# A filter transposed by DMAs out of DRAM and laid out through a DRAM scratch, in place of TensorE and SBUF transposes; first units in narrower column pieces; a new order

## The chip, the cores and the metric

The kernel runs on one core of one Trainium2 chip. The metric is the device time of one execution in microseconds (us), as the median of several runs. Times on the profiled execution are counted from the start of its span. PE is TensorE, DVE is VectorE, ACT is ScalarE, POOL is GpSimd, and SP is the engine that issues most of the DMAs. SP, like every engine, works through its own instructions in order: an instruction that waits holds up all that stand behind it on that engine.

## What is computed

All tensors are bf16. `S` is 2048 time steps and `D` is 512 channels; the hidden width of the gated block is 1792.

```python
xn = layernorm(A_q)                                   # over D
k_shift[s] = sum over j<4 of A_k[s-j] * A_shift_k[:, j]
kv = k_shift * A_v
y  = causal convolution over time of kv with A_ssm_k  # by FFT of length 2S, each channel its own filter
y  = y + kv * A_ssm_D
g  = silu( (gelu(xn @ w_gate) * (xn @ w_up)) @ w_down )
out = A_q + (xn * y) * g
```

`A_ssm_k` is the filter: 512 channels by 2048 time steps in DRAM, a row per channel. All other long inputs have a row per time step.

## The kernel before, in words

**The convolution.** Time step s is split as 16 p + t: p is the partition (128 of them), t one of 16 slots. A first stage (`stage1_h`, `stage1_k`; the matmuls with F1 at L618) transforms over the partitions for each t: two 128x128 weights per slot of 512 channels. Its result is written to a DRAM scratch, ZH for the filter and ZK for kv, and read back regrouped (BH, BK). A second stage (`h_stage2`, `spectrum`, 32x32 tiles at L1028) completes the transform, multiplies the two spectra on DVE (L1091; HS and HW are the filter's spectrum and its swapped copy), transforms back and writes ZI. The last stage reads ZI as BI and multiplies with G1.

**The filter's way into the first stage.** The first stage needs the filter with a row per time step. `load_h` loads the filter as it lies in DRAM, four DMAs of 512 KB into Hn, one for each 128 channels. Two of the four are turned by PE: `h_transpose` (L878) transposes 32-bit pairs of elements against the identity ident32, and ACT or DVE copies the result from PSUM to HTr (L609, L612). The other two are permuted by ACT into HP (L609, four instructions) and then turned by two DMA transposes from SBUF to SBUF, HTD<-HP at L899, issued by SP. So the filter has two halves from here on, "H" and "J", with 16 stores of 256 KB to ZH: those of H are issued by ACT, those of J by SP. `half1` (eight pieces of 256 columns) serves the upper slots of the H half. The staging tiles of these stores lie in X and G.

**The gated block.** The time steps are done in four quarters q of 512 rows (slots 4q to 4q+3). `ln` does the statistics on DVE (L821, L822), the root on POOL (L831, L832) and the normalised rows XN on DVE (L835). `xn_transpose` turns them to xnT: for q 0 and 1 by PE (L854) with a copy by ACT, for q 2 and 3 by DMA (L846). `unit(q, m)` does hidden block m of 128: four matmuls with Wg and four with Wu over 512 columns, a gelu on ACT (L1137) and a product on DVE (L1140) to HT. For q = 0 and m below N_HALF = 2 the unit is done in two pieces of 256 columns (L1128, L1130). `down(q)` multiplies HT with Wd.

**What sets the order.** Each step is a task, added by `S.add` (or `op`), and numbered in the order in which the code adds it. The string SEQ is the order in which the tasks are emitted, written as these numbers; a "b" chooses the second engine of a task that has a choice. Each engine so gets its instructions in the order of SEQ, and PE and SP wait where their data is not there yet. ORDER only sets in what sequence the load tasks are numbered. Waits follow from overlapping reads and writes of the same memory (`Trk`); `after=` adds to them in the plan. The constants in `Sched` and LOAD_NS belong to the plan alone.

The weights Wg and Wu come in four pieces (units 0 and 1, 2 to 5, 6 to 9, 10 to 13). x01 and x11 are the loads of slots 0 and 1 of A_q, x22 that of slots 2 and 3, x1 to x3 those of the later quarters. PE begins with 11 matmuls on zeros (`warm_up`), before the first data lands.

Of the kernel before, what the change touches and what calls it, by code (L numbers as in the profile page):

```python
# [6 lines left out]
BF16 = mybir.dt.bfloat16  # L7
# [6 lines left out]
S_LEN = 2048  # L14
# [11 lines left out]
ORDER = "x01 h0 x11 h1 x22 w0 w1 h2 h3 D0 w2 s0 k0 v0 x1 w3 k1 v1 d0 d1 k2 v2 k3 v3 x2 x3"  # L26
SEQ = (
# [25 lines left out]
LOAD_NS = {("x0_", 262144): 1400.0, ("x0_", 131072): 450.0, 262144: 900.0, 524288: 1350.0, ("x", 524288): 2100.0, ("h", 524288): 1300.0, ("wg", 524288): 1550.0, ("wu", 524288): 1450.0, 917504: 2620.0, ("sk", 524288): 1500.0, 344064: 1250.0, 46080: 350.0, 3072: 100.0, 1024: 200.0}  # L53
W_XT, W_SW, W_BK, W_BH, W_ZI, W_BI, W_ZK, W_MI, W_G1 = 1665000, 600000, 555000, 703000, 333000, 640000, 490000, 740000, 222000
NC_PAIRS = 4
SMALL = 1.15 * 262144
T_FWD = 219.0
T_INV = 438.0
N_HALF = 2
# [232 lines left out]
class Sched:  # L292
# [10 lines left out]
    EARLY, TAKEN, SHARED, WAIT = (0.0, 1.0), 1400.0, 46000.0, 3300.0  # L303
    LANDS = (3150.0, 3490.0, 5770.0)
# [40 lines left out]
    def run(self):  # L345
# [5 lines left out]
        for name in SEQ.split():  # L351
# [13 lines left out]
            if eng == "loads":  # L365
                free[eng] = t.start + dur * (self.EARLY[1] if t.start < self.EARLY[0] else 1.0)
                if n_loads < len(self.LANDS):
                    free[eng] = self.LANDS[n_loads] - self.LOAD_LAT
                n_loads += 1
                t.end = free[eng] + self.LOAD_LAT  # L370
            elif t.nbytes:
                en = t.end
                if en < self.SHARED:
                    free["loads"] += self.TAKEN
                pipe = max(pipe, en + self.DMA_LAT / 2) + t.nbytes / (self.SHARE_BW if en < self.SHARED else self.DMA_BW)
                t.end = pipe + self.DMA_LAT / 2 + (self.WAIT if en < self.SHARED else 0.0)
# [22 lines left out]
def build_kernel(nc, A_q, A_k, A_v, A_shift_k, A_ssm_k, A_ssm_D, B_w_gate, B_w_up, B_w_down, out):  # L399
    with ExitStack() as es0:  # L400
# [31 lines left out]
        ident32 = new("ident32", [128, 128], FP32)  # L432
# [49 lines left out]
        def quarter(T, j):  # L482
            return T[:, j:j + 2, :].rearrange("p x (y d) -> p (x y) d", d=256).rearrange("p (r c) d -> p r c d", c=2)
# [42 lines left out]
        R_id, R_id32 = res("ident", ident[:]), res("ident32", ident32[:])  # L526
# [8 lines left out]
        R_AST = {x: [res(f"AST{x}{j}", a) for j, a in enumerate(ast[x])] for x in "HJK"}  # L535
# [8 lines left out]
        R_Hn = [res(f"Hn{k}", Hn[:, k, :]) for k in range(KD)]  # L544
        R_HTr = [[res(f"HTr{t}_{k}", HTr[:, t, 256 * k:256 * (k + 1)]) for k in range(2)] for t in range(NT // 2)]
        R_HP = [res(f"HP{h}", HP[:, 8 * h:8 * h + 8, :, :]) for h in range(2)]
# [740 lines left out]
```

## Time and profile before

| | us |
|---|---|
| median of 3 runs (lowest, highest) | 196.97 (196.69, 197.29) |
| the profiled execution's own time | 195.77 |
| its span | 194.0 |
| PE busy in the span | 187.5 |
| DVE, ACT, POOL busy | 159.8, 125.5, 14.0 |
| end of PE's warm-up on zeros | 5.84 |
| end of PE's last matmul | 190.25 |

"Busy" is the time in which an engine had at least one instruction under way. The span leaves out 1.77 us of the execution's own time, ahead of its first and behind its last instruction. In rows by line, the last columns are the busy time, the mean ns of one instruction and the idle time of its engine just before them. In rows of the timeline, the first two columns are the start and the length of a run of like instructions, and "x8" is how many. In rows of the windows, each engine has its busy time and its count; the last three columns are the granted clock, the mean busy share of the 16 DMA engines (over 1 where transfers overlap) and the GB/s that they moved. The granted clock is 1.00 in every window of this execution.

### The profile page before, as it was taken

What the parts mean: (1) busy time and instruction counts of PE and PEld (TensorE: products, weight loads), DVE (VectorE), ACT (ScalarE), POOL (GpSimd) and SP (SyncE); (2) the same over time, 40 slices, a digit from 0 to 9 for tenths busy, and PEclk for the clock granted to TensorE, in tenths of its full rate; (3) what the DMA queues carried; (4) which work ended last, traced back from release to release, by engine and by line L of the source; (5) the groups of instructions that cost most, each with busy time, mean ns of one, the idle gap of its engine ahead of it and who ended that gap; (6) DMA issues with size and microseconds to landing.
All of it is one profiled execution on the core that took longest, in us unless ns stands there. A gap on an engine that the chain in (4) does not pass through costs nothing.

```text
span 194.0 us, 3492 instructions
## 1 busy us (share of the span) xinstructions
PE 187.5 (97%) x1364; PEld 85.0 (44%) x1377; DVE 159.8 (82%) x245; ACT 125.5 (65%) x170; POOL 14.0 (7%) x32
## 2 busy tenths in 40 slices
PE   7799999999998999999999999999999999999993
PEld 2594544444443444443434433433444434444442
DVE  7599699998999993977788789878897963588993
ACT  6787999979876978868648767756577531222121
POOL 6412420000000000020300000000000000000000
PEclk9999999999999999999999999999999999999999
DMA  5999999999999859999999991893714344939333
GB/s 165 327 322 349 377 403 315 188 217 375 368 363 355 242 210 231 384 345 283 277 306 221 318 312 41 291 332 106 237 37 184 105 150 135 402 109 363 126 139 135
DMA packets 46102, 49.19 MB, mean 254 GB/s; under 512 B 12803, under 2 KB 39943, under 8 KB 46086
## 3 DMA queue, kind: packets, MB, share of 16 engines
q1 hardware_dynamic: 37510, 42.67, 69.8%
q10 hardware_dynamic: 8576, 6.29, 10.1%
q8 instruction: 11, 0.18, 0.4%
q14 instruction: 5, 0.04, 0.1%
HBM read 27.39 MB, written 14.68 MB: 217 GB/s over the span
## 4 chain that ended last, share of the span: by engine, by line
PE 87%; DMA 7%; ACT 2%; issue 1%; SPq 1%; DVE 1%
PE psall L618 80%; PE psall L1028 5%; DMA Hn<-in_A_ssm_k_dram 3%; DMA ZH<-X 3%; SPq L590 1%; PE psall L854 1%; ACT G L609 1%; PE psall L878 1%; ACT X L609 1%; ACT ASX L609 0%; ACT GE L1137 0%; DVE G L1175 0%; DVE G L1174 0%; ACT G L1172 0%
## 5 line engine op out<-in xcount | busy, mean ns | idle before, releaser
L618 PE MATMUL psall<-xnT,Wu 128*128 128x512 bf16 (+1 forms) x232 | 55.8, 372 | 0.0
L618 PE MATMUL psall<-xnT,Wg 128*128 128x512 bf16 (+1 forms) x232 | 55.3, 372 | 0.0
L618 PE MATMUL psall<-Wd,HT 128*128 128x512 bf16 (+2 forms) x231 | 50.8, 366 | 0.7 <-issue 0.5
L1140 DVE TENSOR_TENSOR HT<-psall,GE 128x512 bf16<-128x512 f32 x54 | 36.7, 685 | 15.2 <-PE psall L618 13.6
L1137 ACT ACTIVATE GE<-psall 128x512 bf16<-128x512 f32 x54 | 31.7, 601 | 12.6 <-PE psall L618 12.2
L618 PEld LDWEIGHTS psall<-Wd,HT 128*128 128x128 bf16 x238 | 22.4, 98 | 25.9 <-issue 1.1
L618 PEld LDWEIGHTS psall<-xnT,Wu 128*128 128x128 bf16 x232 | 21.6, 98 | 25.9 <-issue 3.8
L618 PEld LDWEIGHTS psall<-xnT,Wg 128*128 128x128 bf16 x232 | 21.9, 98 | 25.3 <-issue 1.3
L609 ACT ACTIVATE X<-psall 128x1024 bf16<-128x1024 f32 (+1 forms) x18 | 15.1, 846 | 3.8 <-DMA ZH<-X 3.3
L609 ACT ACTIVATE HS<-psall 128x1024 bf16<-128x1024 f32 x14 | 13.7, 1022 | 4.2 <-PE psall L1028 4.2
L1164 ACT ACTIVATE G<-psall 128x512 bf16<-128x512 f32 x12 | 7.0, 597 | 12.8 <-PE psall L618 12.4
L1011 DVE TENSOR_TENSOR KAC<-KAC,KTM 128x2048 bf16<-128x2048 bf16 x12 | 14.6, 1218 | 0.1
L1009 DVE TENSOR_TENSOR KTM<-KK,SKB 128x2048 bf16<-128x2048 bf16 x12 | 14.6, 1217 | 0.0
L609 ACT ACTIVATE BO<-psall 128x1024 bf16<-128x1024 f32 x9 | 9.1, 1023 | 8.2 <-PE psall L1028 7.7
L821 DVE BATCH_NORM_STATS2 stats<-X 128x6 f32<-128x512 bf16 x16 | 10.3, 677 | 3.9 <-DMA X<-in_A_q_dram 3.9
L609 ACT ACTIVATE KB<-psall 128x1024 bf16<-128x1024 f32 x11 | 11.0, 1021 | 3.6 <-PE psall L1028 3.6
L609 ACT ACTIVATE AST<-psall 128x1024 bf16<-128x1024 f32 x12 | 12.3, 1031 | 1.2 <-PE psall L618 1.0
L612 DVE CAST BO<-psall 128x1024 bf16<-128x1024 f32 x7 | 8.5, 1223 | 3.7 <-PE psall L1028 3.7
L1172 ACT ACTIVATE G<-psall 128x512 bf16<-128x512 f32 (+2 forms) x5 | 2.6, 512 | 13.1 <-PE psall L618 13.1
L1091 DVE TENSOR_TENSOR HW<-KB,HW 128x1024 bf16<-128x1024 bf16 x16 | 10.9, 682 | 0.0
L1091 DVE TENSOR_TENSOR HS<-KB,HS 128x1024 bf16<-128x1024 bf16 x16 | 10.8, 682 | 0.0
L618 PE MATMUL psall<-V,F 128*128 128x512 bf16 x30 | 8.8, 379 | 0.4 <-ACT ASX L609 0.3
(83 smaller groups left out, 172.2 us busy)
## 6 DMA issues: line engine op xcount, KB each, us to landing
BH<-ZH SPq DMA_DIRECT2D x8, 512.0 KB, 6.3
HW<-HS SPq DMA_DIRECT2D x16, 256.0 KB, 2.9
BK<-ZK SPq DMA_DIRECT2D x8, 512.0 KB, 5.1
ZI<-BO ACTq DMA_DIRECT2D x16, 256.0 KB, 2.9
BI<-ZI SPq DMA_DIRECT2D x8, 512.0 KB, 4.1
ZK<-AST SPq DMA_DIRECT2D x6, 512.0 KB, 3.7
Hn<-in_A_ssm_k_dram SPq DMA_DIRECT2D x4, 512.0 KB, 8.4
KK<-in_A_k_dram SPq DMA_DIRECT2D x4, 512.0 KB, 8.8
```

Source lines behind the costliest of these rows:

```text
L609: return h.activation(o, i, ACTF.Copy, scale=scale)
L612: return h.tensor_copy(o, i)
L618: return h.matmul(o, lhsT=l, rhs=r, start=st, stop=sp)
L821: t_stats[t] = op([("DVE", 670.0)], lambda e, h, t=t: h.bn_stats(stats[:, t, :], X[:, t, :]), r=[bX[q][t % 4]], w=[bst[t]], rr=[R_X[t]], w ...
L1009: op([("DVE", dur)], lambda e, h, j=j, m=m: h.tensor_tensor(KTM[:, m.slot, :, :], kk(j), sk(j), ALU.mult), r=need + [bSKB[j], a], w=[m], r ...
L1011: op([("DVE", dur)], lambda e, h, m=m: h.tensor_tensor(KAC[:, a.slot, :, :], KAC[:, a.slot, :, :], KTM[:, m.slot, :, :], ALU.add), r=[m], ...
L1028: trk.op("PE", lambda h: h.matmul(ps(s, i)[b, :], lhsT=wt(col)[a, :], rhs=data(col)[a, :], start=n < 16, stop=n >= len(todo) - 16, tile_po ...
L1091: return hd.tensor_tensor(o, flat(KB, kb[h]), o, ALU.mult)
L1137: op([("ACT", act(512))], lambda e, h: h.activation(GE[:, g.slot, :], bank(pg), ACTF.Gelu_apprx_tanh), r=[pg], w=[g], rr=lambda: R_bank(pg ...
L1140: op([("DVE", dve(512, 1))], lambda e, h: h.tensor_tensor(HT[:, q % 2, m, :], bank(pu), GE[:, g.slot, :], ALU.mult), r=[pu, g], w=[bHT[q][m]],
L1164: op([("ACT", act(n))], lambda e, h, g=g, pc=pc: h.activation(g, pc(), ACTF.Tanh, scale=0.5), r=[p], w=[bt], rr=lambda p=p: R_bank(p), ww= ...
L1172: op([("ACT", act(n))], lambda e, h, g=g, pc=pc: h.activation(g, pc(), ACTF.Silu), r=[p], w=[bt], rr=lambda p=p: R_bank(p), ww=rg, after=z ...
```

## The change

The whole filter is now turned by four DMA transposes out of DRAM. Each takes 512 time steps of all 512 channels into HT1 (`load_h`, i below 4; "hT"). HT1 then has 128 consecutive time steps on the partitions. Four plain stores write it to a new DRAM scratch HD, with a row per time step ("HDst"), and four plain loads read HD back with time step 16 p + t on partition p ("HFld"), into HF, which lies in the upper halves of XN and X. All twelve are issued by SP, 512 KB each. HDst waits for its transpose to land; every HFld waits for all four stores. The filter's first stage becomes the same code as kv's: 16 slots of 512 channels, two slots to a store of 512 KB with rows of 1 KB, all eight issued by SP. `h_transpose`, the HP permutation, `half1`, ident32 and the split in two halves go. The staging tiles of ZH lie in G now.

N_HALF goes from 2 to 6: in the first quarter, units 0 and 1 are done in pieces of 128, 128 and 256 columns and units 2 to 5 in two pieces of 256. Some `after` conditions change, and SEQ is a new order throughout.

Read as names, SP's order in the new SEQ is: x01, x11, wg0, wu0, x22, x1, wu1, wg1, taps and halo, wu2, wg2, k0, wu3, k1, wg3, hT2, v0, hT0, hT1, hT3, HDst2, HDst0, HDst3, HDst1, v3, k2, HFld2, v1, MI (second), HFld0, MI (first), D, d0, HFld3, HFld1, d1, ZH5, ZH4, v2, ZH1, ZK3, k3, ZH7, ZH3, G1, ZK0, ZK1, ZH2, ZH0, ZH6, ZK2, x3, BH0, ZK4, BH1, x2, ZK5, ZK7, ZK6, BH2, HW0, BK0, BK1, BK2, then the DMA transpose of xnT for q = 3. In the old SEQ the stretch that ends with BK0 is: x01, x11, h0, x22, h1, wg0, wu0, x1, wg1, halo, D, wu1, h2, wg2, taps, k0, wu2, wg3, wu3, h3, v3, v0, k1, HTD0, HTD1, v2, k2, d0, v1, d1, MI (first), k3, ZK0, ZJ4, x2, ZJ6, MI (second), ZK1, ZJ1, ZJ3, ZJ7, G1, ZJ2, ZJ5, ZK3, ZJ0, ZK4, x3, ZK2, BH0, BH1, ZK5, ZK6, ZK7, BH2, HW0, BK0 (d0 and d1 are the two loads of Wd; ZJ are the J half's stores to ZH).

On PE the new order begins, after the warm-up: transposes of XN slots 0 and 1; units 0 and 1 on the first 128 columns (four groups of four matmuls); Wg of unit 1 on the second 128; Wu of unit 2 on the first 256; Wu of unit 1 and Wg of unit 0 on the second 128; the transpose of slot 3; and so on. On DVE, behind the first normalised rows: statistics of slots 3 and 2, the product of unit 0's first piece, the statistics of slot 4, the product of unit 1's first piece, the statistics of slot 7, then the normalised rows of slots 2 and 3.

The diff, cut to its core:

```diff
-N_HALF = 2
+N_HALF = 6
+PARTS = ([(0, 1), (1, 2), (2, 4)], [(0, 2), (2, 4)])
...
-        Hn = at("Hn", [128, KD, S_LEN], BF16, g_at)
-        HTr = at("HTr", [128, NT // 2, DM], BF16, kk_at - 16384)
-        HP = at("HP", [128, NT, 2, 128], BF16, kk_at - 8192)
-        HTD = at("HTD", [128, NT, 2, 128], BF16, xn_at + 8 * 1024)
+        HT1 = at("HT1", [128, NT, DM], BF16, g_at)
+        HF = [at(f"HF{i}", [128, NT // 2, DM], BF16, a) for i, a in enumerate((xn_at + 8192, xn_at - 8192))]
...
-        ast = {"H": [quarter(X, j) for j in (8, 10, 12, 14)], "J": [quarter(T, j) for T, j in ((X, 12), (X, 14), (G, 4), (G, 6))],
+        ast = {"H": [G[:, j:j + 4, :].rearrange("p (r c) d -> p r c d", c=2) for j in (4, 8, 12)],
                "K": [AST[:, j, :, :, :] for j in range(2)] + [ASX[:]]}
+        HD = nc.dram_tensor("HD", [S_LEN, DM], BF16, kind="Internal")
...
-        def load_h(k, ring):
-            load(f"h{k}", Hn[:, k, :], h_dr[:, k, :], [R_Hn[k]], [bHn[k]], 524288, ring)
+        h_in, h_dt = [], [dsem(f"d_ht{i}") for i in range(4)]
+
+        def load_h(i):
+            if i < 4:
+                h_in.append(S.add([("loads", 3200.0)], lambda e: trk.dma("SP", lambda h: h.dma_start(out=HT1[:, 4 * i:4 * i + 4, :], in_=A_ssm_k[:, 512 * i:512 * i + 512], transpose=True), h_dt[i], w=[R_HT1[i]]), w=[bHT1[i]], nbytes=W_XT))
+            elif i < 8:
+                j, sem = i - 4, dsem(f"d_hs{i}")
+                dst = bass.AP(HD, 512 * j * DM, [[DM, 128], [128 * DM, 4], [1, DM]])
+                h_in.append(S.add([("loads", 1500.0)], lambda e: dma("SP", dst, HT1[:, 4 * j:4 * j + 4, :], sem, [R_HT1[j]], [R_HD[j]]), r=[bHT1[j]], w=[bHDr[j]], nbytes=524288))
+            else:
+                j, sem = i - 8, dsem(f"d_hr{i}")
+                src = bass.AP(HD, 4 * j * DM, [[NT * DM, 128], [DM, 4], [1, DM]])
+                h_in.append(S.add([("loads", 1350.0)], lambda e: dma("SP", HF[j // 2][:, 4 * (j % 2):4 * (j % 2) + 4, :], src, sem, R_HD, R_HF[4 * j:4 * j + 4]), r=bHDr, w=[bHF[j]], nbytes=524288))
...
-        def h_transpose(k):
-...
-        for k in range(2):
-            h_transpose(k)
-...
+        bFold = B("fold")
+        op([("DVE", 420.0)], lambda e, h: h.tensor_tensor(HF[0][0:1, 0, :], HF[0][0:1, 0, :], Drow[:], ALU.add),
+           r=[bHD, bHF[0]], w=[bFold], rr=[R_D, R_HF[0]], ww=[R_HF[0]])
...
+        def stage1(x, u):
             a = B(f"A{x}{u}", pAST[x])
+            for i in range(2):
+                p, t = B(f"ps1{x}{u}_{i}", pC), 2 * u + i
+                data, rd, bd = (V[:, t, :], R_V[t], [bKV[u // 2]]) if x == "K" else (HF[t // 8][:, t % 8, :], R_HF[t], [bHF[u // 2]] + ([bFold] if t == 0 else []))
...
-                for i in range(2):
-                    c = slice(256 * i, 256 * i + 256)
+                for i, (j0, j1) in enumerate(PARTS[0 if m < 2 else 1]):
+                    c, n = slice(128 * j0, 128 * j1), 128 * (j1 - j0)
```

More of the change, by code (lines that the diff above doesn't have):

```diff
@@ L25 @@
 N_WARM = 11
-ORDER = "x01 h0 x11 h1 x22 w0 w1 h2 h3 D0 w2 s0 k0 v0 x1 w3 k1 v1 d0 d1 k2 v2 k3 v3 x2 x3"
+ORDER = "x01 x11 w0 x22 w1 h0 h1 h2 h3 h4 h5 h6 h7 h8 h9 h10 h11 D0 w2 s0 k0 v0 x1 w3 k1 v1 d0 d1 k2 v2 k3 v3 x2 x3"
 SEQ = (
[22 rows of a table removed]
[22 rows of a table added]
 )
@@ L543, in build_kernel @@
         R_KTM = [res(f"KTM{j}", KTM[:, j, :, :]) for j in range(1)]
-        R_Hn = [res(f"Hn{k}", Hn[:, k, :]) for k in range(KD)]
-        R_HTr = [[res(f"HTr{t}_{k}", HTr[:, t, 256 * k:256 * (k + 1)]) for k in range(2)] for t in range(NT // 2)]
-        R_HP = [res(f"HP{h}", HP[:, 8 * h:8 * h + 8, :, :]) for h in range(2)]
-        R_HTD = [res(f"HTD{h}", HTD[:, 8 * h:8 * h + 8, :, :]) for h in range(2)]
+        R_HT1 = [res(f"HT1_{i}", HT1[:, 4 * i:4 * i + 4, :]) for i in range(4)]
+        R_HF = [res(f"HF{t}", HF[t // 8][:, t % 8, :]) for t in range(NT)]
+        R_HD = [trk.free_res(f"HD{i}") for i in range(4)]
         R_SKR = res("SKR", SKR[:])
@@ L564, in build_kernel @@
         R_BI = [res(f"BI{j}", BI[:, j, :, :]) for j in range(4)]
-        R_Z = {"H": [trk.free_res(f"ZH{t}") for t in range(NT)],
+        R_Z = {"H": [trk.free_res(f"ZH{t}") for t in range(NT // 2)],
                "K": [trk.free_res(f"ZK{t}") for t in range(NT // 2)],
@@ L631, in build_kernel @@
         bWd = [B(f"Wd{i}") for i in range(2)]
-        bHn = [B(f"Hn{k}") for k in range(KD)]
-        bHTr = [[B(f"HTr{k}_{h}") for h in range(2)] for k in range(2)]
-        bHP, bHTD = [[B(f"{x}{h}") for h in range(2)] for x in ("HP", "HTD")]
+        bHT1, bHDr, bHF = [[B(f"{n}{i}") for i in range(4)] for n in ("HT1_", "HDr", "HF")]
         bHD = B("HD")
@@ L638, in build_kernel @@
         bKV = [B(f"KV{i}") for i in range(4)]
-        bZ = {x: [B(f"Z{x}{i}") for i in range(8 if x == "K" else 16)] for x in "HKI"}
+        bZ = {x: [B(f"Z{x}{i}") for i in range(16 if x == "I" else 8)] for x in "HKI"}
         bG = [B(f"G{j}") for j in range(8)]
@@ L732, in build_kernel @@
         bFM = B("fm")
-        S.add([("DVE", 700.0)], lambda e: f_mul(), r=[bcq], w=[bFM])
+        S.add([("DVE", 900.0), ("POOL", 1200.0)], lambda e: f_mul(e), r=[bcq], w=[bFM])
         S.add([("DVE", 310.0)], lambda e: f_phase(), r=[bFM], w=[bFP])
@@ L888, in build_kernel @@
-        for k in range(2):
-            h_transpose(k)
-        h_perm, h_dtr = [], []
-        d_htd = [dsem(f"d_htd{hf}") for hf in range(2)]
-        for hf in range(2):
-            for k in range(2):
-                h_perm.append(op([("ACT", act(1024, True)), ("DVE", dve(1024, 1))], lambda e, h, hf=hf, k=k: copy(e, h, HP[:, 8 * hf:8 * hf + 8, k, :], Hn[:, 2 + k, :].rearrange("p (a t) -> p t a", t=NT)[:, 8 * hf:8 * hf + 8, :]),
-                                 r=[bHn[2 + k]], w=[bHP[hf]], rr=[R_Hn[2 + k]], ww=[R_HP[hf]]))
@@ L896, in build_kernel @@
-        for hf in range(2):
-            def dtr(e, hf=hf):
-                o = HTD[:, 8 * hf:8 * hf + 8, :, :].rearrange("p t k d -> p (t k) d")
-                trk.dma("SP", lambda h: h.dma_start(out=o, in_=HP[:, 8 * hf:8 * hf + 8, :, :].rearrange("p t k a -> p (t k a)"), transpose=True), d_htd[hf], r=[R_HP[hf]], w=[R_HTD[hf]])
-            h_dtr.append(S.add([("loads", 3600.0)], dtr, r=[bHP[hf]], w=[bHTD[hf]], nbytes=W_XT))
-        HT0 = HTr[0:1, 0, :].rearrange("p (d c) -> p c d", c=2)[:, 0, :]
@@ L902, in build_kernel @@
-        HD0 = HTD[0:1, 0, :, :].rearrange("p k d -> p (k d)")
-        bFold, bFoldD = B("fold"), B("foldD")
-        op([("DVE", 420.0)], lambda e, h: h.tensor_tensor(HT0, HT0, Drow[:, 0:256], ALU.add),
-           r=[bHD, *[bHTr[k][0] for k in range(2)]], w=[bFold], rr=[R_D, *R_HTr[0]], ww=R_HTr[0])
-        op([("DVE", 420.0)], lambda e, h: h.tensor_tensor(HD0, HD0, Drow[:, 256:512], ALU.add),
-           r=[bHD, bHTD[0]], w=[bFoldD], rr=[R_D, R_HTD[0]], ww=[R_HTD[0]])
+        bFold = B("fold")
@@ L912, in build_kernel @@
         xn_transpose(0)
[L915 to L916 removed]
+        s1_tasks = []
+        zh_tasks = []
         zk_tasks = []
[L919 to L927 removed]
@@ L976, in build_kernel @@
-        d_ast = {x: [dsem(f"d_ast{x}{j}") for j in range(len(ast[x]))] for x in "HJK"}
-        for x in "HJ":
-            for u in range(NT // 2):
-                stage1_h(x, u)
-        S.behind(x_late[0], zh_tasks["H"])
-        S.behind(x_late[1], zh_tasks["H"] + zh_tasks["J"])
-        zh_tasks = zh_tasks["H"] + zh_tasks["J"]
+                dst = bass.AP(ZK if x == "K" else ZH, 4 * u * DM, [[32 * DM, 128], [DM, 4], [1, DM]])
+                dma(e, dst, ast[x][a.slot].rearrange("p r c d -> p (r c) d"), d_ast[x][a.slot], [R_AST[x][a.slot]], [R_Z[x][u]])
@@ L985, in build_kernel @@
+            (zk_tasks if x == "K" else zh_tasks).append(S.add([("SP", ISSUE)] + ([("ACT", 350.0)] if x == "H" else []), st, r=[a], w=[bZ[x][u]], nbytes=W_ZK))
+        d_ast = {x: [dsem(f"d_ast{x}{j}") for j in range(len(ast[x]))] for x in "HK"}
+        for u in range(NT // 2):
+            stage1("H", u)
+        for t in x_late:
+            S.behind(t, zh_tasks)
         kshift_tasks = []
```

119 lines of the change are left out of this document (29 added, 90 removed), and 44 rows, old and new, of the table SEQ.

## The prediction

> **What bounds the kernel now.** I read the busy times first, then who PE waited for, then PE's timeline at the start, then the DMA views.
>
> ```profile
> PE 187.5 (97%) x1364; PEld 85.0 (44%) x1377; DVE 159.8 (82%) x245; ACT 125.5 (65%) x170; POOL 14.0 (7%) x32
> ```
>
> PE is the bound. Of the 6.5 us without PE, 1.0 lies before the warm-up and 3.7 behind the last matmul (190.25 to 194.0). The table of waits, asked for PE, has nearly all the rest:
>
> ```profile
> PE psall L878 <- DMA Hn<-in_A_ssm_k_dram: 0.8, 2, 0.6
> ...
> PE psall L618 <- ACT HTr L609: 0.2, 1, 0.2
> ```
>
> These 1.0 us lie between 5.84 and 9.40, as PE's timeline shows (0.19, 0.23, 0.59). From 9.40 to the end PE hardly stands still.
>
> ```profile
> 6.04 1.27 PE L878 MATMUL psall<-ident,Hn 128*128 128x128 f32 x8 [0.19 <-DMA Hn<-in_A_ssm_k_dram]
> 7.14 0.61 PE L854 MATMUL psall<-ident,XN 128*128 128x128 bf16 x8
> 7.98 0.83 PE L618 MATMUL psall<-HTr,F 128*128 128x256 bf16 x6 [0.23 <-ACT HTr L609]
> ...
> 9.40 1.17 PE L878 MATMUL psall<-ident,Hn 128*128 128x128 f32 x8 [0.59 <-DMA Hn<-in_A_ssm_k_dram]
> ```
>
> So the time after is PE's work plus PE's waits, and a few us of ACT or DVE saved (HP's 8.4, HTr's 3.8) are worth nothing by themselves: PE did not wait for them. The filter's work is also what fills PE here, while A_q's rows are on their way. The last views are the DMA's: windows (us, PE, PEld, DVE, ACT, POOL, clock, DMA share, GB/s) show it full from 2 us on.
>
> ```profile
> 44.00:52.00 8.00, 7.95 (x38) 3.62 (x38) 7.24 (x9) 7.32 (x11) 0.00 (x0) 1.00 1.07 380
> 10.00:32.00 22.00, 21.95 (x143) 12.78 (x143) 20.07 (x35) 19.12 (x29) 5.38 (x8) 1.00 1.06 364
> 34.00:39.00 5.00, 4.95 (x25) 2.36 (x25) 5.00 (x7) 5.00 (x8) 0.00 (x0) 1.00 1.08 189
> ```
>
> **PE's work.** Durations per matmul from the chain and the timeline: 0.219 us for 512 columns, 0.1225 for 256, 0.055 for 128 (the transposes at L854):
>
> ```profile
> 170.94 10.74 PE psall L618 x49
> ```
> ```profile
> 12.38 1.47 PE L618 MATMUL psall<-xnT,Wg 128*128 128x256 bf16 x12
> ```
> ```profile
> 11.01 0.22 PE psall L854 x4
> ```
>
> (10.74/49, 1.47/12, 0.22/4; the first and third are pieces of the chain, the second is of the timeline.) Out: the 16 transposes of L878, 1.27 + 1.17 = 2.44; the 16 half-width first-stage matmuls, 1.96; 32 gate and up matmuls of 512 columns, units 2 to 5, 7.01. In: 48 more of 256 columns, 5.88 (units 2 to 5 bring 64, units 0 and 1 lose 16); 32 of 128 columns, 1.76; 8 first-stage matmuls of 512, 1.75. Sum: -2.0. Work behind the warm-up was 190.25 - 5.84 - 1.0 = 183.4 and becomes 181.4. PE ends at 5.84 + 181.4 + W = 187.2 + W, with W all of PE's later waits. **W = 3.0 is break-even.** The tail behind PE's end (3.7) keeps its tasks.
>
> **The start.** PE runs through its new order in 2.5 us behind the warm-up: two transposes of XN (0.44), seven groups on 128 columns (7 x 0.22), one on 256 (0.49). Then it needs the transpose of slot 3, at 8.3 at the earliest. Slot 3 comes with x22. DVE's timeline shows when that lands:
>
> ```profile
> 7.99 0.69 DVE L821 BATCH_NORM_STATS2 stats<-X 128x6 f32<-128x512 bf16 x1 [1.27 <-DMA X<-in_A_q_dram]
> 8.72 0.18 DVE L822 BATCH_NORM_AGGREGATE mv<-stats 128x2 f32<-128x6 f32 x1
> ...
> 9.91 0.41 DVE L835 TENSOR_SCALAR XN<-X,mv 128x512 bf16<-128x512 bf16 x1 [0.21 <-POOL mv L832]
> ```
>
> x22 was behind 0.13 + 0.13 + 0.52 MB of loads (h0 among them); now it is behind 0.13 + 0.13 + 0.26 + 0.26, as much. I keep 7.95. DVE's new order then holds four statistics at 0.69, two aggregates at 0.18, two small products (0.25 each, estimated below the 0.41 of 256 columns) and two normalised rows at 0.41 before slot 3 is ready: 4.4 us, 12.4. Wu's piece for units 2 to 5, on PE just before, is 1.0 MB later in the queue than x22; at the 320 GB/s or so of 4 to 10 us it lands near 11, Wg's near 12.5. All three say that PE resumes at about 12.5: **W = 4.2 from the start alone.** What hid these waits was the filter's PE work, now gone; the narrow pieces only use what has landed.
>
> **The DMA.** In: four transposes of 0.52 MB and eight plain transfers of 0.52 MB for HD. Out: four plain loads (Hn) and two transposes (HTD). That is 2.1 MB plain and two transposes more. ZH keeps its 4.2 MB in longer rows. A transpose's price from both sides, from the DMA view of 34 to 39 us, where HTD's run:
>
> ```profile
> GB/s 215 145 63 41 45 39 39 39 31 98 264 295 289 289 287 293 289 291 293 291 144 18 8 119 201 197 197 287 352 291 233 133 156 168 227 258 238 246 236 236
> ```
> ```profile
> q1 hardware_dynamic: 2571, 0.65, 82.7%
> ```
>
> It runs at 290 GB/s when it runs (1.8 us), but with the pauses SP's queue moved 0.65 MB in 82.7% of 5 us, 157 GB/s (3.3 us). From DRAM none is shown: from a plain load's 1.4 up to the 5.7 that SP spent on the issue of one xnT transpose (L846). I take 2.5, between the two ends of the nearest rows. [...]
>
> The place to test is BK0, the first read of kv's spectrum: behind it stand all stores of ZH and ZK, and PE's matmuls on it (`spectrum`, L1028) wait for it with everything after them. Before:
>
> ```profile
> 85.82 2.11 SPq L590 DMA_DIRECT2D BK<-ZK  x3
> ```
> ```profile
> BK<-ZK SPq DMA_DIRECT2D x8, 512.0 KB, 5.1
> ```
>
> So it landed near 90.9, and PE took it at 91.64 without a wait: no slack to give away. After: 6.7 MB up to wg3 take until 21.5 (2.5 MB by 10 us, then 364 GB/s). Then come, in SP's order up to BK0, the four transposes and the 0.59 MB of MI and G1 at 210 GB/s (the same 2.5 us), 12.8, and 21.2 MB of plain transfers (40.5 pieces of 0.52) at 380 GB/s, 55.9. With 1.5 to land: 91.7. PE's work ahead of BK0 (old 91.64, less its 1.0 of waits, less 0.9 by the counts above plus five more Wd matmuls) puts its matmuls at 89.7 + W. That alone asks for W = 2.0, less than the start does. But the same sum for the old order (10.5 MB by 32 us; then 7.8 for transposes, 11.4 for 3.4 MB of half-row ZH stores at ACT's queue's 299 GB/s, 31.0 for 11.8 MB plain, 1.5) gives 83.7, and it was 90.9: 7.2 us went in pauses, where SP stood before an instruction whose data was not ready. The new order has such places too: HDst3 waits for a transpose with v3 and k2 behind it; HFld2 waits for all four HD stores, with v1, MI, D and d0 behind it; v2 and k3 stand behind ZH and ZK stores that wait for evictions, and DVE's fourth k-shift waits for k3. With half of the 7.2, W = 5.6; with all, 9.2. I take W midway between the start alone and half the pauses: **W = 4.9**, PE's end at 192.1, a span of 195.9, 1.9 above the old one.
>
> The profiled execution took 195.77, 1.20 below the median of 196.97; both orders are compared on one execution, so 1.9 goes on the median: **198.9 us**. The chance is 0.44, with 198.2 (the start alone) to 199.6 (half the pauses) as this case's own range.
>
> **The rivals.**
>
> *All pauses recur.* For it: the old order lost 7.2 us to them, and the new one has more places where SP waits. Against it: more loads lie queued ahead of those places. W = 9.2: span 200.2, 203.2 us. Chance 0.16.
>
> *Out of DRAM a transpose is much dearer*, 5.7 us: four times 3.2 more, W about 14.8, 208.8 us. Only the 7.22 and 4.16 us of SP on xnT speak for it, and these were issued into a full queue. Chance 0.05.
>
> *No change:* W between 2.4 and 3.6, when x22 lands an us earlier and BK0 is in time; 197.0 us. Chance 0.12.
>
> *Faster:* x22 is the place. At 6.0, when h0 landed before, slot 3 is ready at 10.5 and W = 2.2, if the weights come by then: 196.2 us; with the old waits of 1.0, 195.0. It decides from W = 2.4, x22 before 6.2. For it: what lies ahead of x22 are smaller loads. Against: they are as many bytes. [...] Chance 0.23.
>
> **The numbers.** A measurement of this kernel can tell about 0.3% (0.6 us) from no change. Faster by more: 0.23; within: 0.12; slower: 0.44 + 0.16 + 0.05 = 0.65. The range leaves out the dear transpose, a part of the pauses' upper end and the fastest start: 195.4 to 203.4.
>
> **What would show it.** PE's timeline from 5.84 to 13: an idle of about 4 us in front of slot 3's transpose or of unit 2. L878 gone, PE busy lower by about 2. In the DMA view, hT landings of 3 to 7 us and no GB/s gap behind them. PE's waits: DMA BK, BH or Wd named with some us means the queue's pauses; none means that the start alone counted. Wrong if PE resumes before 11, or if PE waits 6 us and more somewhere behind 40 us.

## The result and the profile after

The changed kernel takes 207.79 us (median of 4 runs, 205.96 to 208.12) against 196.83 us before (4 runs beside it, 196.37 to 197.29): 1.0538 times as long, with a 95% interval of 1.0471 to 1.0605. The prediction said 198.9 us, between 195.4 and 203.4. The sign was right, the size was not: 11.0 us more instead of 1.9. The interval leaves some 1.3 us open to either side, and so much hangs on every difference from the change below. The profiled execution took 208.0 us, its span is 206.2 us.

The line of busy times, against PE's 187.5 of 194.0 us before:

```profile
PE 191.8 (93%) x1401; PEld 88.0 (43%) x1401; DVE 156.2 (76%) x245; ACT 120.6 (58%) x169; POOL 12.9 (6%) x31
```

PE is idle for 14.4 us instead of 6.5 and busy 4.3 us longer. ACT and DVE have 4.9 and 3.6 us less to do, and the time did not fall for it, as the prediction said. The table of waits for PE (us in total, times, longest) names the idle time:

```profile
PE psall L612 <- DMA Wu<-in_B_w_up_dram: 2.9, 1, 2.9
PE psall L612 <- ACT G L603: 2.9, 1, 2.9
PE psall L612 <- DMA Wd<-in_B_w_down_dram: 2.7, 1, 2.7
PE psall L853 <- DVE XN L834: 1.6, 2, 1.1
```

The rows for Wu and XN lie in the start, which went much as forecast. PE's timeline (start, length, what; in brackets the idle time just before and what ended it):

```profile
5.97 0.40 PE L853 MATMUL psall<-ident,XN 128*128 128x128 bf16 x4 [1.09 <-DVE XN L834]
...
11.87 1.46 PE L612 MATMUL psall<-xnT,Wu 128*128 128x256 bf16 x8 [2.91 <-DMA Wu<-in_B_w_up_dram]
```

PE resumes at 11.87 (the forecast had 12.5), held by Wu's second piece. The other two long waits, for Wd and for ACT's copy to G, stand at 58 to 69 us, where the forecast had none. The windows (us, PE, PEld, DVE, ACT, POOL, granted clock, DMA share, GB/s) show what came with the waits:

```profile
10.80:11.87 1.07, 0.00 (x1) 0.01 (x1) 1.07 (x3) 0.00 (x0) 0.00 (x0) 0.50 1.05 333
11.87:17.60 5.73, 5.73 (x38) 4.72 (x39) 4.76 (x11) 1.26 (x3) 0.92 (x1) 0.52 1.08 292
57.90:60.70 2.80, 0.11 (x2) 0.02 (x2) 1.32 (x2) 1.81 (x3) 0.00 (x0) 1.00 1.07 389
...
62.00:65.40 3.40, 3.40 (x9) 1.27 (x9) 2.95 (x3) 0.00 (x0) 0.00 (x0) 0.53 0.98 309
65.90:68.80 2.90, 0.10 (x1) 0.00 (x0) 2.81 (x4) 1.02 (x1) 0.00 (x0) 0.97 1.02 417
68.80:72.30 3.50, 3.44 (x9) 1.26 (x10) 0.00 (x0) 3.07 (x4) 0.00 (x0) 0.54 1.04 424
```

With each of the three long waits the granted clock falls to a half for 3.4 or 6.8 us, and PE's matmuls take nearly twice as long (five of 512 columns 2.34 us from 69.69, 1.24 from 72.36). At half speed 5.73, 3.40 and 3.44 us of PE are worth half of that: some 6.3 us lost. Before, the clock was 1.00 throughout. From 72.3 us on PE has no long wait again, so the loss lies before. In both waits in the middle the DMA is full (share 1.07 and 1.02, 389 and 417 GB/s), so the transfers are late, not idle. Just ahead of the first it was not full: from 52 to 58 us it was busy for 67% of the time and moved 177 GB/s.

Why they are late, the windows that the prediction shows of before help to tell. There they moved 380 (44 to 52 us), 364 (10 to 32) and 189 GB/s (34 to 39, where the old transposes ran). Now, with 24 to 32 beside them:

```profile
44.00:52.00 8.00, 8.00 (x39) 3.63 (x37) 7.45 (x9) 5.95 (x10) 0.00 (x0) 1.00 1.04 279
10.00:32.00 22.00, 20.13 (x148) 14.77 (x149) 18.23 (x36) 9.64 (x22) 4.68 (x7) 0.84 1.09 272
24.00:32.00 8.00, 8.00 (x55) 4.49 (x54) 6.95 (x11) 5.26 (x10) 0.00 (x0) 1.00 0.96 191
34.00:39.00 5.00, 5.00 (x25) 2.28 (x24) 4.84 (x6) 1.82 (x4) 0.00 (x0) 1.00 1.07 303
```

The first two are lower, the third is higher. While the filter is transposed (24 to 32 us) the DMA is busy 96% of the time and moves 191 GB/s. SP's queue (start, length of the issue, what) shows the rest:

```profile
15.55 10.03 SPq L774 DMA_TRANSPOSE HT<-in_A_ssm_k_dram  x1
...
26.25 8.60 SPq L774 DMA_TRANSPOSE HT<-in_A_ssm_k_dram  x3
...
52.95 1.23 SPq L964 DMA_TRANSPOSE MI<-TFA  x1
...
54.71 0.40 SPq L584 DMA_DIRECT2D Wd<-in_B_w_down_dram  x1
...
56.98 3.04 SPq L584 DMA_DIRECT2D ZH<-G  x2
...
99.05 2.09 SPq L584 DMA_DIRECT2D BK<-ZK  x3
```

The first half of Wd, before:

```profile
40.62 0.51 SPq L590 DMA_DIRECT2D Wd<-in_B_w_down_dram  x1
```

SP stands 18.6 us on the four transposes. Behind them everything is late: the first half of Wd is issued at 54.71 (40.62 before), after SP has waited 4.9 us for the other MI transpose to land, and behind that wait the DMA runs low (52 to 58 us); ZH's stores start at 56.98 and block ACT, which needs their staging tiles back (ACT's timeline):

```profile
67.78 4.23 ACT L603 ACTIVATE G<-psall 128x1024 bf16<-128x1024 f32 x4 [8.06 <-DMA ZH<-G]
```

The read BH0 is issued at 84.00 (72.83 before), BK0 at 99.05 (85.82 before). BK0 landed 5.7 us after its issue, at 104.7 (90.9 before). The queue came out 11 to 14 us behind.

### The profile page after: what moved, and what is told of

It is laid out like the page before. It is cut to its first block, busy times and chain, and to the rows that moved or that the text cites. A ratio compares the mean times of both kernels' runs of the same rounds, so it can differ in the third digit from the quotient of the medians.

```text
span 206.2 us, 3566 instructions
## 1 busy us (share of the span) xinstructions
PE 191.8 (93%) x1401; PEld 88.0 (43%) x1401; DVE 156.2 (76%) x245; ACT 120.6 (58%) x169; POOL 12.9 (6%) x31
## 4 chain that ended last, share of the span: by engine, by line
PE 84%; DMA 9%; ACT 3%; SPq 1%; DVE 1%; issue 0%; ACTq 0%
PE psall L612 78%; DMA ZH<-G 5%; PE psall L953 5%; DMA Wu<-in_B_w_up_dram 4%; ACT G L603 3%; SPq L584 1%; PE psall L853 1%; ACT GE L1062 0%; DVE G L1100 0%; DVE G L1099 0%; ACT G L1097 0%; ACTq L173 0%
## 5 line engine op out<-in xcount | busy, mean ns | idle before, releaser
L612 PE MATMUL psall<-xnT,Wu 128*128 128x512 bf16 (+2 forms) x256 | 57.1, 358 | 2.9 <-DMA Wu<-in_B_w_up_dram 2.9
L612 PE MATMUL psall<-xnT,Wg 128*128 128x512 bf16 (+2 forms) x256 | 57.2, 361 | 0.4 <-ACT xnT L603 0.4
L612 PE MATMUL psall<-Wd,HT 128*128 128x512 bf16 (+2 forms) x238 | 54.3, 375 | 2.7 <-DMA Wd<-in_B_w_down_dram 2.7
L1065 DVE TENSOR_TENSOR HT<-psall,GE 128x512 bf16<-128x512 f32 x50 | 33.4, 685 | 10.2 <-PE psall L612 9.9
L612 PEld LDWEIGHTS psall<-xnT,Wg 128*128 128x128 bf16 x256 | 24.6, 101 | 24.9 <-issue 0.9
L603 ACT ACTIVATE G<-psall 128x1024 bf16<-128x1024 f32 x16 | 16.1, 1024 | 9.7 <-DMA ZH<-G 8.1
L1091 DVE SCALAR_TENSOR_TENSOR G<-G,psall 128x512 bf16<-128x512 bf16 x12 | 8.2, 682 | 14.6 <-ACT G L1089 14.6
L603 ACT ACTIVATE KB<-psall 128x1024 bf16<-128x1024 f32 x14 | 13.8, 1023 | 4.7 <-PE psall L953 3.2
L936 DVE TENSOR_TENSOR KAC<-KAC,KTM 128x2048 bf16<-128x2048 bf16 x12 | 14.6, 1219 | 0.1
L934 DVE TENSOR_TENSOR KTM<-KK,SKB 128x2048 bf16<-128x2048 bf16 x12 | 14.6, 1217 | 0.1
L612 PE MATMUL psall<-HF,F 128*128 128x512 bf16 x32 | 10.0, 429 | 2.9 <-ACT G L603 2.9
L1053 ACT ACTIVATE GE<-psall 128x256 bf16<-128x256 f32 (+1 forms) x14 | 4.6, 355 | 10.7 <-PE psall L612 4.8
```

The source lines that it names most:

```text
L603: return h.activation(o, i, ACTF.Copy, scale=scale)
L612: return h.matmul(o, lhsT=l, rhs=r, start=st, stop=sp)
L934: op([("DVE", dur)], lambda e, h, j=j, m=m: h.tensor_tensor(KTM[:, m.slot, :, :], kk(j), sk(j), ALU.mult), r=need + [bSKB[j], a], w=[m], r ...
L936: op([("DVE", dur)], lambda e, h, m=m: h.tensor_tensor(KAC[:, a.slot, :, :], KAC[:, a.slot, :, :], KTM[:, m.slot, :, :], ALU.add), r=[m], ...
L1053: op([("ACT", act(n))], lambda e, h, p=p2[0], g=g2, c=c: h.activation(GE[:, g.slot, c], bank(p)[:, c], ACTF.Gelu_apprx_tanh), r=[p2[0]], w ...
L1065: op([("DVE", dve(512, 1))], lambda e, h: h.tensor_tensor(HT[:, q % 2, m, :], bank(pu), GE[:, g.slot, :], ALU.mult), r=[pu, g], w=[bHT[q][m]],
```

## The experiments

The theories, by name. **The start:** the idle start and its halved clock cost the time. **The transposes:** four transposes out of DRAM are slow and hold SP. **The scratch:** the eight transfers of HD cost the time by their bytes. **The chain:** not the bytes but the wait of the reads for the stores. **The clock:** the half clock behind the waits costs what its rows show. **The slack:** the old order had slack for a part of the added bytes, as the prediction held. The letters in the quoted expectations hold only within each of them. Each ratio is against runs of the kernel before on the same chip beside it: 196.31 us (start masked, Wd earlier, plain loads, short warm-up), 196.35 (the two without scratch, MI ahead of x3, split units), 196.55 (no scratch with fillers, reads unchained, MI behind x2, eight stores) and 196.00 (four stores, fillers in all waits).

### The start masked, and Wd earlier

Fillers in the long wait of the start (in code they stand ahead of unit 2's first Wu group):

```diff
+    for i in range(14): mm(bank, ident, ident broadcast to 512 columns)   # overwritten
     for kd in range(KD): mm(bank, Wu ..., xnT ...)
```

> The changed kernel with 14 matmuls of 512 columns on the identity (3.0 us of work whose result is overwritten) on PE just before the first matmul that waited 2.9 us for Wu's second piece. Theory A (a stretch of about 3 us without PE work halves the granted clock afterwards): the clock stays at 1.0 between 10.8 and 17.6 us, the 5.7 us of half-rate work there become 2.9, and the kernel takes about 205 us, 2.9 less than 207.8. Rival B (the clock falls for another reason, the short matmuls or the DMA's load): the clock falls all the same and the time stays at 207.8 or rises by up to 0.3.

208.08 us, 1.0612 [1.0546, 1.0677]. The clock at the start stayed at 1.00, and nothing was gained: PE's waits behind it grew to 3.0 (Wd), 1.6 (HF) and 4.5 us (ACT G). The theory of the start falls as the cause of the loss: what the start loses or saves is masked by the transfers behind it.

SP's order with Wd's two loads earlier, and MI's first transpose (the second to be issued) behind the last read of HD:

```diff
-k2, HFld2, v1, MI (second), HFld0, MI (first), D, d0, HFld3, HFld1, d1
+k2, d0, HFld2, v1, d1, MI (second), HFld0, D, HFld3, HFld1, MI (first)
```

> The changed kernel with three DMAs moved in SP's order: the two loads of Wd ahead of the first read of HD and behind v1, and the second of MI's transposes (which waited 4.9 us for the first one to land, with Wd's loads behind it) to the place behind the last read of HD. Theory A (SP's order, a stand behind a wait, made Wd late): PE's wait of 2.7 us for Wd and the half clock behind it (1.7 us lost) go; if the late burst of HD reads, Wd and ZH stores also made the ZH store of 10.8 us, the wait of 2.9 us behind it and its 1.7 us go too: 198.8 to 203.4 us. Rival C (the DMA is simply full with the transposes and the HD traffic): another transfer is late by as much, and the time stays above 206.

205.12 us, 1.0459 [1.038, 1.0539]. The wait for Wd is gone; PE waits 6.1 us for HF instead. SP's queue shows why:

```profile
46.15 0.60 SPq L584 DMA_DIRECT2D Wd<-in_B_w_down_dram  x1
46.79 7.78 SPq L964 DMA_TRANSPOSE MI<-TFB  x1
54.61 0.58 SPq L584 DMA_DIRECT2D HF<-HD  x1
```

With 0.9 MB of Wd queued right ahead, the transpose holds SP for 7.78 us (2.50 in the change), and HF's reads behind it come late. A wait was moved. The 2.7 us by which the median is lower lie between the two forecasts, and the intervals overlap.

### The transposes and the scratch taken away

The four transposes replaced by plain loads of as many bytes:

```diff
-dma_start(out=HT1[:, 4*i:4*i+4, :], in_=A_ssm_k[:, 512*i:512*i+512], transpose=True)
+dma_start(out=HT1[:, 4*i:4*i+4, :] as (p, t d), in_=A_ssm_k[128*i:128*i+128, :])
```

> The changed kernel with its four DMA transposes replaced by plain loads of the same 512 KB each, so the filter goes in untransposed; the rest is unchanged. Rival C (the transposes' price fills the DMA queue): about 1.1 us less for each of four plus SP's long issues, so HD is ready 5 to 8 us sooner, the waits at 58 and 66 us go, and the time falls to about 199 to 201 us. Theory A: SP still stands 4.9 us at MI's second transpose with Wd behind it; the waits shrink only by what the queue is ahead by then, and the time stays at 203 or more.

200.84 us, 1.0238 [1.0184, 1.0293]: 7.0 us less than the change. The DMA's window of this run beside the change's 191 GB/s:

```profile
24.00:32.00 8.00, 8.00 (x51) 4.40 (x50) 7.63 (x11) 7.38 (x13) 0.00 (x0) 1.00 1.04 399
```

The wait for Wd is gone, the one of 2.9 us for ACT's copy to G is not. 7.0 us for four is 1.75 us each above a plain load's 1.4: about 3.1 us a transpose, if the kernel's time follows the queue. The landings say nearly the same: the last of the four landed 12.8 us behind wg3 in the change (25.75 to 38.52, with v0 in between) and 6.3 us behind it here (25.54 to 31.86), which is 1.6 us more each, 2.9 in all. The theory of the transposes holds for this part.

The scratch left out: the transposes write HF directly, HD's stores and reads issue nothing.

```diff
-dma_start(out=HT1[:, 4*i:4*i+4, :], in_=A_ssm_k[...], transpose=True)
+dma_start(out=HF[i//2][:, 4*(i%2):4*(i%2)+4, :], in_=A_ssm_k[...], transpose=True)
-dma(HD <- HT1) x4; dma(HF <- HD) x4
```

> The changed kernel without the way through the scratch: the four DMA transposes write straight to the tile that the first stage reads, and the four stores to HD and the four loads from it are left out, so the filter's time steps lie in the wrong rows. Theory C (the DMA's time and its chain of landings from the transposes to the first stage is the bound between 22 and 76 us): 4.2 MB, some 11 us of transfers, and two landings of 4 to 7 us leave the chain; the waits at 58 and 66 us go and the time falls to 196 to 199. Theory D (only the transposes' own slowness matters, since it is what the plain-load run took away): the time stays within 2 us of 207.8.

198.02 us, 1.0097 [1.006, 1.0134]: 9.8 us less than the change. The waits of PE:

```profile
PE psall L612 <- DMA Wu<-in_B_w_up_dram: 1.7, 1, 1.7
...
PE psall L612 <- ACT G L603: 0.9, 2, 0.5
```

The theory of the scratch holds. No long wait in the middle is left, and in the profiled execution (197.25 us) the clock is 1.00 throughout (in four of the other five its mean is 0.99), though the DMA still moves only 205 GB/s from 24 to 32 us and SP stands even longer on the four transposes, 10.70 and 9.56 us. So SP's stand alone does not cost the time. PE's busy time in this run is 186.7 us: with the same warm-up of 4.85 us and the full clock, the change's PE work is 0.8 us below the 187.5 of before.

Both edits at once:

> The same without the scratch, and the transposes replaced by plain loads of the same bytes as well. Theory C: every wait behind the start goes; PE's end is then 187.2 plus the start's waits (about 4) and the half clock behind them (up to 2.9), 197 to 200 us. If it is under 196, the start's waits were worth less than theirs in the forecast.

198.88 us, 1.0134 [1.0102, 1.0166]. The two gains, 7.0 and 9.8, do not add up to 16.8: once the stretch from 22 to 72 us has room, only the start is left, where PE waits 2.2 us for Wu and 1.4 for XN and the clock then halves. So the bytes of the scratch and the slowness of the transposes press on one bound, the DMA's time there, and taking away either frees much of it.

The same with the 14 fillers of the first experiment at the start:

> The run without the scratch and with plain loads for the transposes (198.9, no wait on PE behind the start), with 14 matmuls on the identity ahead of the start's wait for Wu. If half clock behind the start's wait is what that run still paid (its profile: 3.4 us at half, from 11.2 to 14.6), up to 1.7 us go: 197.2 to 198. If the start's wait alone counts, 198.9 as without.

197.89 us, 1.0072 [1.0043, 1.01]. The window of 11.0 to 14.6 us of the run without fillers, and of this one:

```profile
11.00:14.60 3.60, 3.41 (x27) 3.09 (x28) 3.60 (x9) 0.48 (x2) 0.00 (x0) 0.53 1.05 292
```
```profile
11.00:14.60 3.60, 3.17 (x35) 2.34 (x34) 3.60 (x9) 0.87 (x2) 0.00 (x0) 1.00 1.06 290
```

27 matmuls at 0.53 against 35 at 1.00 in as long. Here, where no transfer masks it, the fillers gain 1.0 us; the two intervals just miss each other. That it is the clock is not shown by every execution: without fillers, the one with a mean clock of 1.00 took 199.25 us, the other three 198.49 to 199.06. Even so, with nothing left of what the change adds to the transfers, the new start and order stay 1.3 us above before.

### The chain, and SP's order

The reads of HD take the same bytes from A_v instead, and so wait for no store:

```diff
-src = bass.AP(HD, 4*j*DM, ...)     # waits for the four stores
+src = bass.AP(A_v, 4*j*DM, ...)    # waits for nothing
```

> The changed kernel with the same four stores to HD, but with the four reads taking the same shape and bytes from A_v in DRAM, so they wait for no store (the filter read in is not the filter). All of the DMA's bytes stay; the landing of the stores before the reads goes. Theory F (it is the chain of landings, each 4 to 8 us, that makes it late): the waits at 58 and 66 us shrink and the time falls to 199 to 202. Theory G (it is the bytes and the transposes' rate, the DMA being full): the time stays above 205.

207.49 us, 1.055 [1.0517, 1.0583], as slow as the change: PE's waits are 3.5 (ACT G), 2.6 (Wd) and 0.9 us (HF). The theory of the chain falls as a cause by itself. The edit's reach is short, though: HFld2 is issued at 41.93 instead of 44.01, then MI's first transpose holds SP for 5.13 us instead of 2.50, and from 52.7 on the queue is where it was. The wait for the transposes ahead of HDst, and the chain with MI out of the way, were not tried.

Two more orders of SP's queue, with both MI transposes moved back behind ZH's stores:

```diff
-v1, MI (second), HFld0, MI (first), D, ... ZK2, x3, ... x2, ...
+v1, HFld0, D, ... ZK2, MI, MI, x3, ... x2, ...     # the first
+v1, HFld0, D, ... ZK2, x3, ... x2, MI, MI, ...     # the second
```

> The changed kernel with the two DMA transposes of MI moved in SP's order from among the reads of HD to the place ahead of x3's load, behind the ZH stores. Theory E (a DMA transpose is issued slowly and holds SP while the transfers ahead of it drain, so the loads behind it come late: SP spent or waited 2.5 + 4.9 + 1.2 us there): the remaining reads of HD and Wd's loads are issued some 6 us sooner, the waits for Wd and the ZH store shrink to under 2 us in total, and the time falls to 200 to 203. Rival (the DMA is full whatever SP does): the time stays above 206.

207.69 us, 1.0587 [1.0545, 1.063]: the first order gains nothing, though the DMA now moves 383 GB/s from 52 to 56 us, against 152 in the change.

> The changed kernel with MI's two DMA transposes put behind x2's load in SP's order (about 87 us), so neither the reads of HD and Wd's loads nor x3's load stand behind them. In the run with MI ahead of x3 the wait for Wd had gone and a wait of 4.4 us for DVE had come at about 87 us. Theory E2 (that wait was x3 held by MI: DVE stands at the statistics of slot 14, and the copies out of PSUM behind it): it goes here, and the time falls to 201 to 204. Theory C (the chain from the transposes to the first read of ZH is late whatever stands in between): another wait takes its place and the time stays above 205.

205.92 us, 1.0487 [1.0444, 1.053]. With MI ahead of x3 the wait for Wd is gone, and PE waits 4.4 us from 86.3 on for DVE's product in G, since DVE stands 6.15 us for x3, whose load is behind MI. With MI behind x2 that wait went as well, and smaller ones took its place (1.6 for ACT G, 1.4 and 0.5 for HS). Three orders gave 0.1 to 2.7 us of the 11, none of them clear of the intervals: the order chooses which load is late.

### The kernel before with more to transfer

Eight stores of 512 KB to a scratch that nothing reads, behind the filter's second transpose in the kernel before, and nothing else:

```diff
+if hf:
+    for i in range(8): dma("SP", HD rows 512*i ..., Hn[:, i % 4, :])
```

> The kernel before with eight more stores of 512 KB (Hn to a scratch in DRAM that nobody reads) on SP behind the second HTD transpose: 4.2 MB more, as much as HD's traffic, that nothing waits for but the reuse of Hn's memory and the queue behind it. Theory G (the DMA is full up to the spectrum, with the 4 to 5 us of slack that the forecast's sum left): some 11 us of transfers more, 4 to 8 us slower, 200 to 204. Theory F (bytes without a chain are absorbed by the 3 to 7 us of pauses in the old queue): under 198.5.

209.27 us, 1.0652 [1.0611, 1.0693]: 12.7 us more, beyond either forecast. And with four (`range(4)`), the change's own 2.1 MB:

> The kernel before with 4 more stores of 512 KB (2.1 MB, the plain bytes that the change adds) to an unused scratch, issued behind the second transpose of the filter: half the dose of the run with eight (+12.7 us). Theory 'no slack at all': the transfers take 2.1 MB at 380 GB/s = 5.5 us longer and PE waits for them: 202.4 us, up to 203 with a halved clock. Theory 'a slack of some us, then each byte counts' (the prediction held half of the 7.2 us of pauses to be slack): 5.5 less 3.6 = 1.9 us, 198.5 us; full slack: 196.9.

202.90 us, 1.0354 [1.031, 1.0398]: 6.9 us more, where 5.5 us of transfers were added. The theory of the slack falls in its size: 3.6 us or more of slack would have left 198.5 us or less. DVE's timeline has the place, in this run and, below it, before:

```profile
54.28 1.23 DVE L1010 TENSOR_TENSOR KAC<-KK,SKB 128x2048 bf16<-128x2048 bf16 x1 [5.91 <-DMA KK<-in_A_k_dram]
```
```profile
48.50 1.22 DVE L1005 TENSOR_TENSOR KAC<-KK,SKB 128x2048 bf16<-128x2048 bf16 x1
```

and PE's what follows from it:

```profile
57.30 1.58 PE L619 MATMUL psall<-xnT,Wg 128*128 128x512 bf16 x4 [4.75 <-DVE HT L1145]
```

Before, DVE began this k-shift at 48.50 without a wait, so nothing looked late. Its load k2 was issued at 39.99 and landed at 46.4, 2.1 us ahead of the need: that was the slack. With the four stores k2 was issued 5.5 us later, at 45.47, and landed at 54.25, 7.9 us later; so DVE began 5.8 us later. The stores cost the queue more than their 5.5 us: from 39 to 54 us it moved 304 GB/s, at which 2.1 MB take 6.9. PE stood 4.75 us for DVE's product in HT, which began at 56.55, two rows behind this k-shift, and its next matmuls ran at the half clock for 3.4 us (0.71 on average over 56 to 60 us). 4.75 and 1.7 make 6.5 of the 6.6 us by which the span is longer: here the half clock counted in full. With eight stores the same k-shift waited 12.57 us and PE 11.4.

### The halved clock where the transfers bind

The change with fillers in all three long waits:

```diff
+14 matmuls on ident ahead of unit 2's first Wu group
+12 ahead of the first matmuls on Wd
+14 ahead of the filter's slot 7 in the first stage
```

> The changed kernel with matmuls on the identity in PE's three longest waits: 14 of 512 columns ahead of unit 2's first Wu group, 12 ahead of the first matmuls on Wd, 14 ahead of the first-stage matmuls of the filter's slot 7 (3.1, 2.6 and 3.1 us at 0.219 us each). Their results are overwritten; nothing is left out. The granted clock should stay at 1.00. Theory 'the halved clock costs what the rows show' (6.3 us of PE's work): 201.5 us. Theory 'transfers bound this stretch, PE's rate there is masked, except for the last half-rate piece of 68.8 to 72.3 behind which PE no longer waits (1.7 us)': 206 us, between 205.5 and 207; the waits then grow by what PE gains.

208.47 us, 1.0621 [1.0577, 1.0666]. The mean clock rose from 0.967 to 0.992 and the time did not fall. PE's timeline:

```profile
56.92 2.75 PE L612 MATMUL psall<-ident 128*128 128x512 bf16 x12
60.00 1.04 PE L612 MATMUL psall<-Wd,HT 128*128 128x512 bf16 x4 [0.33 <-DMA Wd<-in_B_w_down_dram]
...
63.06 3.19 PE L612 MATMUL psall<-ident 128*128 128x512 bf16 x14
...
69.05 0.60 PE L612 MATMUL psall<-HF,F 128*128 128x512 bf16 x2 [2.37 <-ACT G L603]
```

PE was done with its fillers at 66.3 and still waited until 69.05; in the change it waited until 68.86. The theory of the clock falls as a cost here: the 6.3 us are real in the rows, but the end of that wait is set by ZH's stores. The 1.7 us that I expected from the last piece did not show either, since behind the 2.37 us that PE still waited in front of it the clock was below 1.00 once more (0.84 over 66 to 72, 0.90 over 72 to 80).

### Two smaller questions, on the kernel before

Units 2 to 5 of the first quarter in two pieces of 256 columns, alone:

```diff
-N_HALF = 2
+N_HALF = 6
```

> The kernel before with the matmuls of units 2 to 5 of the first quarter split into two of 256 columns each in the same PSUM bank; all else as before. By the row's 0.1225 against 0.219 us it is 32 times 0.026, 0.8 us slower (ratio 1.004). If splitting costs nothing, 1.000; if the doubled weight loads bind, 2 us and more.

196.71 us, 1.0028 [0.9999, 1.0058], some 0.5 us, at the edge of what is told from nothing. A short warm-up (3 matmuls instead of 11), to see what an idle PE at the start costs where its filter work follows:

```diff
-N_WARM = 11
+N_WARM = 3
```

> The kernel before with 3 warm-up matmuls in place of 11, so PE has nothing to do from about 2.3 to 6.0 us. Theory A: the granted clock is at half in that time and for some us of real work behind it; 2 to 4 us slower than before, 199 to 201. Rival B: the idle stretch costs nothing, since PE's first real work comes at 6.0 either way: 196.8.

196.82 us, 1.0039 [1.0008, 1.007]. PE idled for 3.1 us and the cost was 0.4%. The idle stretch did slow what came behind it: the first eight transposes of L878 took 1.95 us (1.27 before) and the next six first-stage matmuls 1.48 (0.83), though the granted clock reads 1.00 there. It cost little: the 1.0 us that PE waits in that stretch before are gone here.

## Why the prediction was wrong, point by point

**"PE is the bound; the time after is PE's work plus PE's waits."** Right as bookkeeping: the span's 12.2 us more are 7.9 of idle PE, about 6 of halved clock, 0.8 less work and 1.0 less of warm-up (its 11 matmuls took 3.91 us this time, 4.87 before). One reading in it was off, in the table before and in the prediction: 190.25 is the end of the last matmul but a piece of 128 columns; the last one ends at 190.99, so the tail is 3.0 us and not 3.7. The tail is 3.0 after the change too, so the forecast does not hang on it. But the waits are no small term here. From 22 to 72 us the DMA sets the time.

**PE's work, −2.0 us.** It measured −0.8 (186.7 without the scratch against 187.5, both at the full clock). The split is not what is missing: the sum has 0.8 us for it, and alone it cost some 0.5 in the kernel before. Which term was too small by 1.2 us is not shown. Break-even was so nearer W = 1.8.

**The start, W = 4.2.** PE resumed at 11.87 against 12.5, held by Wu as one of the three reasons said. The idle pieces sum to 4.9 us from 4.88 on, where the warm-up ended this time (1.09, 0.49, 0.41, 2.91), and to 3.9 from the 5.84 that the forecast counts from. Another of the reasons came out right by luck: x22 landed at 6.85, 1.1 us before the 7.95 kept, but DVE then stood 1.84 us for x1's rows, and slot 3 was still ready only at 12.6. Right in size, and without effect: filling it changed nothing (208.08). It matters only where the transfers are relieved (198.88 and 197.89 us).

**A transpose, 2.5 us.** Some 3 by the plain-load run (2.9 to 3.1): from 24 to 32 us the DMA moved 191 GB/s with the transposes and 399 with plain loads in their place. The rival with 5.7 us was too dear; that its 208.8 us is near the measured time is luck.

**The failed step: the queue's pauses, taken half as slack.** The prediction had the added transfers right: 2.1 MB, 5.5 us at its 380 GB/s, and two transposes at 2.5, together 10.5. Then it compared its sum for the old order (83.7) with the trace (90.9 at BK0), called the 7.2 us between them pauses, and let the new order keep at most half of them, 3.6 us: "W midway between the start alone and half the pauses". The trace after answers at the same read. BK0 landed at 104.7, 13.0 us behind the sum's 91.7: the pauses came back in full, and 5.8 us more. The queue was 4.1 us behind the sum when the last transpose landed (38.5, against 34.4 from 21.5, four at 2.5, v0's 1.4 and 1.5 to land; 1.6 of it is the transposes' price), and 8.9 more came behind that, SP's 4.9 us for MI among them. And where the old order was tested it had less room than that, 2.1 us at k2. Four stores cost it 6.9 us, eight 12.7. Had the 10.5 us gone on the time undiminished, 207.5 us would have come out, near the measured time in part by chance; at measured prices (6.9, and 6.2 for two more transposes) it is 13.1, less the 0.8 of PE's work. That this stands 1.3 us above the measured 11.0 is within what the interval leaves open.

**The place, BK0.** The prediction tested the queue at one read, long behind the added transfers, and found it nearly in time. The waits came earlier, at loads and stores that it had named only in passing: Wd behind MI, and ZH's staging tiles. It had named its own disproof, a wait of 6 us behind 40; the two waits there are 2.69 and 2.86, 5.6 together, with the halved clock beside them.

**The rival "all pauses recur", 203.2.** It was nearest in cause (PE's waits, W = 9.2, against 10.4 measured: 14.4 less 1.0 ahead of the warm-up and 3.0 behind the last matmul), but it left out that PE's clock was at a half with its three long waits, about 6 us in the rows. By how much the end was later for that is another matter: the fillers show that in the middle this was masked.

**What stays open.** How the 18.6 us of SP on the transposes divide between their own rate and the queue that they were issued into; a kernel with the transposes on a queue of their own was not tried. Which pauses make up the 13.0 us: MI's was taken away, and the time stayed (207.69). And whether a much better order of SP's queue exists: the three that were tried gained 2.7 us at most.

## What to carry to other kernels

A queue that is busy throughout and whose consumers do not wait has not been shown to have slack: add the bytes of the change to the kernel before, as transfers that nothing reads, and see. Read when the loads land, too: one that nobody waited for was only 2.1 us early here. Where the sum of a queue falls short of the trace, the difference is a missing term of the queue, and it is not to be spent on new transfers. Work that was moved from an engine to the DMA was paid for at the DMA's price in that stretch (6.9 us for 2.1 MB, some 3 us for a transpose), and PE work that stood in a start where PE must wait anyway was free here.

## What the runs showed of the hardware

**The granted clock was at a half with some of PE's waits, and with others as long it was not.** In the change it read 0.50 in three stretches, from 10.59 to 17.42, 61.79 to 65.20 and 68.62 to 72.03, the first and the last of which begin while PE waits (2.91 and 2.86 us) and the second 1.1 us behind a wait's end (2.69 us). When the reads were unchained a wait of 2.0 us at the start went with a mean of 0.88 over 10 to 24 us, but behind one of 3.34 us PE's next matmuls took 0.60 us for two and 1.24 for five, as at 1.00. The clock stayed at 1.00 with one of 2.2 us at the start of the plain-load run (8 to 16 us), with one of 2.99 us for Wd with the start masked (56 to 64), and with one of 1.7 us without scratch (10 to 24). The length of a wait alone does not decide it in these runs; what does is not shown. The price was 1.7 us of the span for 3.4 us at half with four stores in the kernel before, where nothing masks it, and none in the middle of the change.

**A DMA transpose held SP for between 1.23 and 10.03 us in the change:** 10.03 for the first of the filter's, 8.60 for the next three together, 2.50 and 1.23 for MI's two. One of MI's took 7.78 with 0.9 MB of Wd queued right ahead. Without the scratch, plain loads in the filter's place held SP for 2.85 us (one) and 2.12 (three), transposes for 10.70 and 9.56. What stands behind a transpose on SP was issued late by that (HF's read behind the 7.78 at 54.61); whether it costs time is another matter (198.02 us without the scratch, with the 10.70 and 9.56).
